# Eight padded projection tiles and 32-row scores in the first of two attention layers, pairs placed by the runs that close in the second

## The chip, the core and the metric

The program runs on one core of a Trainium2 chip. A core has engines that run side by side, each with its own queue of instructions in order: TensorE (PE) multiplies matrices from SBUF into PSUM banks; ScalarE (ACT) evaluates functions, here above all the exponential; VectorE (DVE) does elementwise work, reductions and copies out of PSUM; GpSimd (POOL) does elementwise work in SBUF; SyncE (SP) issues DMA transfers. The metric is the device time of one execution in microseconds. The kernel before took 1752.12 us, the median of three runs from 1749.59 to 1755.61.

## What is computed

Two layers, each an attention block and a token-mixing MLP, over one sequence of 2048 tokens of 640 features. Weights are shared by both layers.

```python
def _A_ref(x, wqkv, wo):                     # B, S, D, H = 1, 2048, 640, 32; Dh = 20
    qkv = (x @ wqkv).reshape(B, S, 3, H, Dh).transpose(2, 0, 3, 1, 4)
    q, k, v = qkv[0], qkv[1], qkv[2]
    scores = jnp.einsum("bhqd,bhkd->bhqk", q, k) * (Dh ** -0.5)
    p = _softmax(scores, axis=-1)
    o = jnp.einsum("bhqk,bhkd->bhqd", p, v)
    return o.transpose(0, 2, 1, 3).reshape(B, S, D) @ wo

def _B_ref(x, w1, b1, w2, b2):               # F = 1536
    h = _layernorm(x, axis=-1)
    u = _gelu(jnp.einsum("bsd,sf->bdf", h, w1) + b1)
    return (jnp.einsum("bdf,fs->bds", u, w2) + b2).transpose(0, 2, 1)

x = x + _A_ref(_layernorm(x), A_wqkv, A_wo)
x = x + _B_ref(_layernorm(x), B_w1, B_b1, B_w2, B_b2)
# and both once more
```

## The kernel before

**Scores and exponentials.** The 32 heads form 8 groups of four. The keys of a group are a tile of `KT` with 128 partitions: head `j` of the group has its 20 features in partitions 32j to 32j+19. Queries stand likewise in `QTq`, one block of 512 queries at a time, four blocks. A *unit* is one query block, one group and 128 keys: four *chunks* of 128 keys by 512 queries, one per head, each one matmul over 20 rows in its own strip of the array (`s_matmul`, lines 733 to 738). A chunk's exponential is done in one of two ways. ScalarE takes tiles of three and of two chunks in turn (`emit_exp`, line 806). VectorE takes chunks two at a time, a *pair*: one step from PSUM to integers (L576), then a polynomial and an addition of exponent bits (L617, L622, L641 or L643), with POOL doing two of the steps where it can (L694, L677). Each layer has 2048 chunks. `ve_admit` (from line 533) decides which chunks become pairs: it picks a unit `n` some way ahead of the cursor, by VectorE's planned backlog.

**Sums over keys.** `emit_PV` (L1466) multiplies the exponentials with the values into one bank `acc`. A *run* is a query block and a group, 16 units; when it closes, VectorE transposes the bank (L843), adds a partial sum where there is one, divides and transposes back (`finish_run`).

**The order is planned.** The Python code writes out every engine's order from modelled costs: `pem["t"]`, `dvm["t"]` and `acm["t"]` are the planned times of TensorE, VectorE and ScalarE. The order is then fixed; on the chip engines wait for one another by semaphores. Between score and value matmuls TensorE gets *fills* (projections, transposes, output and MLP matmuls; `add_fill`, `fill_step`), by priority and subject to gates, each evacuated by VectorE or ScalarE. Where the activity planned in a window of `SPAN_US` is under a floor (`wanting`, line 300), it gets *filler waves*, four matmuls of ones with zeros (L795). A fill matmul of 512 columns and a filler wave count 1 cell, a score chunk 0.25, whatever its rows.

**Hidden projections.** Each strip of 32 partitions has 12 unused ones. The kernel before projects five tiles (`NP`), not eight: the features of groups 5, 6 and 7 lie in the gaps of tiles 0 to 4, as `HIDDEN` says (tile, first gap row, rows, first feature). After the projection, DMAs on SyncE's queue carry them to their places (`carry`, L1215; `move_keys`, `move_queries`). The weights in the gaps are put there once, in the first layer, by 14 POOL copies (`gap_copies`, L1698), for groups 1 to 3 ahead of their first projection. Tile 0 is needed before that; its first projection runs with zeros in the gaps, and a second one of the same columns (`apart_fill`) goes to a separate tile, from where its pieces are moved.

**The opening of the first layer** (`TokenFeed.begin`). Input tiles of 128 tokens are loaded, normalised, transposed (L1357) and projected, four of them for each block of keys. Attention starts with *early runs*: groups 0 to 3 of query blocks 0 and 1, over the keys there are; their partial sums are kept in the key tiles 4 to 7 (`homes`), which can be filled only when the owner's early runs are done. SyncE issues in order: input tiles 0 to 3, the first halves of the key and query weights, half of the value weights, the second halves, input tiles 4 and 5, and the rest as buffers come free. Groups 0 to 3 of the weights are padded by ScalarE, group 4 by VectorE (L1735, L1737).

**The close of a layer** (`end_tiles`). The last two token tiles are finished apart; then the MLP's second product starts (`mixer_head`, L1942, L1955, L1964) with `w2s` blocks loaded ahead (L1977). The MLP's first product adds up in rows of `uacc`; `mid_rows` says for how many of its 12 rows four token tiles are added early.

**The second layer** (`MixFeed`) is fed by the MLP of the first. Until its feed has ended, pairs work in the upper half of `QTq` (`lent`, `new_w`), so fewer are in flight, and queries of groups 4 to 7 wait for it (`given_back`).

## Time and profile before

| quantity | us |
|---|---|
| median of three runs | 1752.12 |
| the profiled execution | 1746.78 |
| its span in the trace | 1745.0 |
| TensorE busy | 1672.1 |
| ScalarE busy | 1658.2 |
| VectorE busy | 1563.2 |
| POOL busy | 598.1 |

The profile is of one execution. A row of a group of instructions gives line, engine, operation, output and input tiles, shape and count, then busy time and the mean of one in ns, then the engine's idle time before them and what ended it. A row of a timeline gives start, duration, engine, line and count; in brackets stands the idle time before it and the work that ended it. A row of stretches gives the stretch, its length, each engine's busy time (PE, weight loads, VectorE, ScalarE, POOL; instructions in parentheses), the granted TensorE clock as a share of full speed, the DMA share and GB/s. Means of overlapping instructions on one engine can add up to more than its busy time.

### The profile page before, as it was taken

To read this page: it belongs to the slowest core of one execution; us is meant where nothing else is said; L and a number is where in the kernel's file an instruction comes from. 1 tells how busy PE (TensorE), PEld (TensorE's weight loads), DVE (VectorE), ACT (ScalarE), POOL (GpSimd) and SP (SyncE) were. 2 spreads that over 40 slices of the span, in tenths; PEclk is the share of its full clock that TensorE was granted. 3 is DMA by queue.
4 is the path that set the end of the run, shared out by engine and by line. 5 is a ranking of instruction groups with operands and counts; after the bars stand their busy time and mean duration, and the time that the engine had idled before them with its cause. 6 is when DMAs were issued, how large, how long until landed. Compare 5 with 4: busy or idle time off the path is not lost.

```text
span 1745.0 us, 44737 instructions
## 1 busy us (share of the span) xinstructions
PE 1672.1 (96%) x18414; PEld 659.0 (38%) x18414; DVE 1563.2 (90%) x2538; ACT 1658.2 (95%) x1488; POOL 598.1 (34%) x966
## 2 busy tenths in 40 slices
PE   8999999999999999999999999999999999999999
PEld 3333333333333344444534333333333333444445
DVE  7699999999999999998658669999999999999973
ACT  8999999999999999999789999999999999999970
POOL 4143333343544333342003113334335443434310
PEclk9999999999999999999999999999999999999999
DMA  5000000010122002023322011001002220211345
GB/s 130 24 13 1 16 14 2 15 39 3 51 60 81 20 28 68 6 76 110 113 81 75 25 57 21 11 2 51 18 15 81 70 62 2 69 53 30 79 121 178
DMA packets 107998, 85.91 MB, mean 49 GB/s; under 512 B 53504, under 2 KB 91952, under 8 KB 107792
## 3 DMA queue, kind: packets, MB, share of 16 engines
q1 hardware_dynamic: 102256, 75.16, 14.9%
q0 software_dynamic: 5536, 7.88, 1.5%
q8 instruction: 144, 2.36, 0.6%
q14 instruction: 62, 0.51, 0.1%
HBM read 55.48 MB, written 23.59 MB: 45 GB/s over the span
## 4 chain that ended last, share of the span: by engine, by line
ACT 48%; issue 22%; PE 21%; DVE 6%; DMA 1%; POOL 1%; SPq 0%; ACTq 0%; DVEq 0%; POOLq 0%
ACT P L806 48%; PE S L736 6%; PE acc L1466 3%; PE ya L1955 2%; PE acc L795 2%; PE misc L1304 1%; PE misc L1108 1%; DVE ey L622 1%; DVE ew L576 1%; PE um L1942 1%; DVE ey L617 1%; PE ya L1964 1%; PE misc L1333 1%; PE yb L1955 1%; PE Dt L1304 1%
## 5 line engine op out<-in xcount | busy, mean ns | idle before, releaser
L806 ACT ACTIVATE P<-S 128x1536 bf16<-128x1536 f32 (+1 forms) x1421 | 1609.2, 1355 | 17.3 <-PE S L736 16.1
L736 PE MATMUL S<-QTq,KT 20*128 20x512 bf16 (+1 forms) x4434 | 575.2, 338 | 55.9 <-ACT P L806 40.0
L694 POOL TENSOR_SCALAR ey<-ew 128x512 f16<-128x512 uint16 x508 | 313.9, 618 | 616.6 <-DVE ey L622 256.2
L736 PEld LDWEIGHTS <-KT 20*128 20x128 bf16 x5136 | 225.7, 91 | 519.7 <-issue 492.8
L795 PE MATMUL acc<-zr,zw 128*32 128x512 bf16 x4928 | 378.3, 382 | 1.2 <-POOL zr L160 1.2
L576 DVE TENSOR_SCALAR ew<-Dt 128x512 int32<-128x512 f32 x524 | 357.2, 682 | 23.3 <-PE Dt L736 14.1
L1466 PE MATMUL acc<-P,Vaug 128*32 128x512 bf16 (+1 forms) x4418 | 371.4, 344 | 0.1
L622 DVE SCALAR_TENSOR_TENSOR ey<-ey,ew 128x1024 int16<-128x1024 f16 x262 | 327.5, 1250 | 2.0
L677 POOL TENSOR_SCALAR Pd<-ew 128x512 int16<-128x512 int16 x304 | 187.2, 617 | 229.9 <-DVE ey L622 73.9
L736 PE MATMUL Dt<-QTq,KT 20*128 20x512 bf16 (+1 forms) x702 | 209.8, 334 | 0.0
L617 DVE TENSOR_TENSOR ey<-ey 128x1024 f16<-128x1024 f16 x273 | 195.2, 715 | 2.2 <-POOL ey L694 0.6
L795 PEld LDWEIGHTS <-zw 128*32 128x32 bf16 x5220 | 129.8, 96 | 116.0 <-issue 63.9
L1466 PEld LDWEIGHTS <-Vaug 128*32 128x32 bf16 x5120 | 104.1, 94 | 183.5 <-issue 169.8
L643 DVE SCALAR_TENSOR_TENSOR Pd<-ew,ey 128x512 int16<-128x512 int16 (+1 forms) x145 | 141.1, 973 | 0.0
L641 DVE TENSOR_TENSOR Pd<-Pd,ey 128x1024 int16<-128x1024 int16 (+1 forms) x197 | 124.0, 630 | 4.8 <-POOL Pd L677 2.8
L1466 PE MATMUL acc<-Pd,Vaug 128*32 128x512 bf16 (+1 forms) x702 | 107.5, 338 | 1.5 <-DVE Pd L641 1.1
L936 POOL TENSOR_TENSOR rstd<-veps,mhalf 128x1 f32<-128x1 f32 x60 | 47.8, 797 | 111.2 <-DVE veps L934 92.8
L1108 PEld LDWEIGHTS <-w1st 128*128 128x128 bf16 x672 | 53.0, 97 | 61.3 <-issue 49.1
L1108 PE MATMUL misc<-x1last,w1st 128*128 128x320 bf16 x384 | 73.0, 302 | 0.0
L1157 PE MATMUL misc<-wo_pad,attnT 128*128 128x320 bf16 x384 | 71.7, 302 | 0.8 <-DVE xin L1169 0.6
L843 DVE STREAM_TRANSPOSE T<-acc 128x512 f32<-128x512 f32 (+1 forms) x82 | 56.9, 694 | 11.9 <-PE acc L1466 11.7
L1108 PE MATMUL misc<-hh,w1st 128*128 128x320 bf16 x280 | 51.4, 301 | 1.4 <-DVE hh L1116 0.6
(157 smaller groups left out, 1200.4 us busy)
## 6 DMA issues: line engine op xcount, KB each, us to landing
w2s<-in_B_w_dram SPq DMA_DIRECT2D x16, 768.0 KB
uacc<-ustg POOLq DMA_DIRECT2D x24, 320.0 KB, 2.5
x1in<-xd SPq DMA_DIRECT2D x24, 320.0 KB
...
```

Of the source, the lines that this page charges most:

```text
L576: nc.vector.tensor_scalar(out=w[:, slot, :], in0=Dt[:, :], scalar1=127.0 * FIX, scalar2=0.0, op0=ALU.add, op1=ALU.max)
L617: nc.vector.tensor_tensor(out=y, in0=y, in1=y, op=ALU.mult)
L622: nc.vector.scalar_tensor_tensor(out=box["t"][:, 0:512 * k], in0=y[:, 0:512 * k], scalar=MANT_C * MANT_K ** 2, in1=frac, op0=ALU.add, op1= ...
L641: nc.vector.tensor_tensor(out=bits, in0=bits, in1=t, op=ALU.add)
L643: nc.vector.scalar_tensor_tensor(out=bits, in0=whole[:, lo:hi], scalar=128.0, in1=t, op0=ALU.mult, op1=ALU.add)
L677: after_vector(nc.gpsimd.tensor_scalar(out=bits, in0=whole, scalar1=128.0, scalar2=0.0, op0=ALU.mult, op1=ALU.add))
L694: return engine.tensor_scalar(out=out_ap, in0=in_ap, scalar1=MANT_K / FIX, scalar2=-MANT_K * MANT_S, op0=ALU.mult, op1=ALU.add)
L736: pe(nc.tensor.matmul(out_ap[:, c0:c0 + w], lhsT=KT[32 * j:32 * j + DH, g, kt * 128:(kt + 1) * 128], rhs=get_QT(st, qb)[32 * j:32 * j + DH ...
L795: pe(nc.tensor.matmul(bank[32 * j:32 * j + 32, 0:w], lhsT=zw[:], rhs=zr[:, :, 0:64].to_broadcast([128, w // 64, 64]), start=start, stop=st ...
L806: nc.scalar.activation(out=P[:, 0:ncs, :].rearrange("p a b -> p (a b)"), in_=St[:, 0:ncs, :].rearrange("p a b -> p (a b)"), func=ACT.Exp, ...
L1108: pe(nc.tensor.matmul(t[:, 0:w], lhsT=w1_of[(p, ft)][:, sti, :], rhs=rows_in[sti][:, c0:c1], start=(sti == 0), stop=(sti == n_in - 1)))
L1466: pe(nc.tensor.matmul(acc[32 * j:32 * j + 32, a0:a0 + w], lhsT=Vaug[:, (kt * H + hh_) * VW:(kt * H + hh_) * VW + 32], rhs=P[:, slot, c0:c0 ...
```

## The change

In the first layer all eight groups are projected as tiles of their own with zeros in the gaps. Tiles 5 to 7 of the weights are in a new pool (`w_over`) that lives as long as the layer. Its scores are matmuls over 32 rows, the 12 rows of zeros included. There are no moves and no separate copy of tile 0 in this layer. At its close `fold` copies the weights of groups 5 to 7 into the gaps of tiles 0 to 4 (14 POOL copies), for the second layer, which keeps five tiles, moves and 20 rows. The second halves of the key and query weights are loaded after input tile 5's normalisation. Groups 4 to 7 are padded by VectorE. ScalarE and VectorE zero the gaps. The order of late groups and the homes of partial sums in the first layer are now 6, 7, 4, 5. `mid_rows` of the first layer is 0.

A score chunk now counts its rows over 128 in the planned activity (0.25 in the first layer, 20/128 in the second), and the floors are per layer, 0.04 lower in the second. In the second layer the unit for a new pair is moved on by the number of closed runs that still have units pending before it, over 1.8.

```diff
-    FLOOR=0.52,
-    FLOOR_RUN=0.68,
+    FLOOR=(0.52, 0.48),
+    FLOOR_RUN=(0.68, 0.64),
...
-    apart = []
+    w_over = []
+
+    def w_of(i, g):
+        return (wk_pad, wq_pad)[i][:, :, g, :] if g < NP else w_over[i][:, :, g - NP, :]
+
+    def quads(ap):
+        return ap.rearrange("p a (j i) -> p a j i", i=32)
+
+    def fold(i, L, tile_, first, n, dim):
+        nc.gpsimd.tensor_copy(out=quads(w_of(i, tile_))[:, :, :, DH + first:DH + first + n],
+                              in_=quads(w_of(i, L))[:, :, :, dim:dim + n])
...
-        homes = {EQ[0]: (4, 6), EQ[1]: (5, 7)}
-        rest = [6, 4, 5, 7]
+        homes, rest = feed.homes, feed.rest
...
-                if len(ve_procs) > 2 or feed.lent and not late and any(q.pair < p - 1 for q in ve_procs):
+                if len(ve_procs) > 2 or feed.nested and not late and any(q.pair < p - 1 for q in ve_procs):
                     return
                 done = backlog(now) + 2 * 1.2 + 4.0 + CFG["VE_MARGIN"]
                 n = max(cursor[0] // NH + max(CFG["VE_LEAST"], math.ceil(done / 1.8)), ve_state["unit"] + 1)
+                if feed.nested:
+                    n += math.ceil(sum(r["closed"] and bool(r["pending"]) and r["pending"][-1] < n
+                                       for r in runs[pv_run[0]:]) / 1.8)
...
-            at = pe_wave("S", cells=0.25) if clash else now
+            at = pe_wave("S", cells=cells_s) if clash else now
...
             for kt, q0, w, c0 in parts:
-                pe(nc.tensor.matmul(out_ap[:, c0:c0 + w], lhsT=KT[32 * j:32 * j + DH, g, kt * 128:(kt + 1) * 128],
-                                    rhs=get_QT(st, qb)[32 * j:32 * j + DH, g, q0:q0 + w], start=True, stop=True,
+                pe(nc.tensor.matmul(out_ap[:, c0:c0 + w], lhsT=KT[32 * j:32 * j + feed.rows, g, kt * 128:(kt + 1) * 128],
+                                    rhs=get_QT(st, qb)[32 * j:32 * j + feed.rows, g, q0:q0 + w], start=True, stop=True,
                                     tile_position=(32 * j, 0)))
...
-
-        def apart_of(i, tile_, tb):
-            return apart[i] if feed.regap and tile_ == 0 and tb == 0 else None
...
-            if feed.regap and L == 5:
-                need.append(("G", 0))
...
             def issue():
                 for tile_, first, n, dim in HIDDEN[L]:
-                    cut = 512 if apart_of(0, tile_, 0) is not None else 0
-                    if cut:
-                        carry(KT[:, L, :], apart[0], 0, cut, first, n, dim)
-                    carry(KT[:, L, :], KT[:, tile_, :], cut, S, first, n, dim)
-                at = moved_at(L, need, 8 if feed.regap and L == 5 else 0)
+                    carry(KT[:, L, :], KT[:, tile_, :], first, n, dim)
...
-        def apart_fill(i, prio):
-            wpad = (wk_pad, wq_pad)[i]
...
-            def evac(t, end, eng):
-                copy_on(eng, apart[i][:], t[:, :], q_scale if i else None)
-
...
         def proj_fill(kind, g, tb, prio, ready, gate=None, fed=False):
-            if g >= NP:
+            if feed.nested and g >= NP:
                 return
-            if kind == "Q" and g >= EG:
+            if feed.nested and kind == "Q" and g >= EG:
                 gate1 = gate
                 gate = lambda: given_back(tb) and (gate1 is None or gate1())
-            wpad, key = (wk_pad, ("K", g, tb)) if kind == "K" else (wq_pad, ("Q", tb, g))
-            if feed.regap:
-                wi = int(kind == "Q")
-                mark = (wi, "gap0") if g == 0 and tb > 0 else (wi, g)
-                gate0 = gate
-                gate = lambda: mark in cx.w_at and (gate0 is None or gate0())
+            wpad, key = (w_of(0, g), ("K", g, tb)) if kind == "K" else (w_of(1, g), ("Q", tb, g))
...
-                    if tb == 0:
+                    if feed.nested and tb == 0:
                         for L in HIDDEN:
                             move_keys(L)
                             move_queries(L, 0)
-                        if feed.regap:
-                            for i in range(2):
-                                apart_fill(i, when(4, 0) - 4)
-                    for g in range(NP):
+                    for g in (*range(EG), *rest):
...
+        if not feed.nested:
+            for i in range(2):
+                for L, parts in HIDDEN.items():
+                    for p in parts:
+                        fold(i, L, *p)
...
-        regap = True
-        lent = False
+        nested = False
+        rows = 32
+        homes = {0: (6, 7), 1: (4, 5)}
+        rest = (6, 7, 4, 5)
...
-        mid_rows = 2
+        mid_rows = 0
...
             load_w(self.wv[:, 0], 2 * D)
-            load_raw(0, 1)
-            load_raw(1, 1)
             for tt in range(4, 6):
                 load_x(tt)
 
             def load_rest():
+                load_raw(0, 1)
+                load_raw(1, 1)
                 load_w(self.wv[:, 1], 2 * D + D // 2)
             landing = {tt: 3.2 + 0.5 * tt for tt in range(4)}
-            landing.update({4: 12.0, 5: 12.5})
+            landing.update({4: 9.5, 5: 10.0})
 
-            def gap_of(i, tile_, first, n):
-                return wpads[i][:, :, tile_, :].rearrange("p a (j i) -> p a j i", i=32)[:, :, :, DH + first:DH + first + n]
-            cx.submit(cx.Proc(0, [(0.2, lambda e, i=i: nc.vector.memset(gap_of(i, 0, 0, GAP), 0.0), 0.0) for i in range(2)], 0.9))
...
-            gaps_at(10.8, [(0, 1)])
-            gaps_at(12.0, [(1, 1), (0, 2), (1, 2), (0, 3), (1, 3)])
-            gaps_at(19.0, [(0, 4), (1, 4)])
-            gaps_at(19.0, [(0, 0), (1, 0)], lambda: ("K", 0, 0) in cx.kready and ("Q", 0, 0) in cx.kready)
+            def pads(i, part):
+                w = (wpads[i][:, :, 0:4, :], wpads[i][:, :, 4:NP, :], w_over[i][:])[part]
+                return w.rearrange("p a g (j i) -> p a (g j) i", i=32)[:, :, :, DH:32]
+            cx.submit(cx.Proc(0, [(0.46, lambda e, i=i: nc.vector.memset(pads(i, 0), 0.0), 0.0) for i in range(2)], 0.9))
 
...
-                              [], 2.1, eng=cx.acm))
+                              [((0.2, 0.42)[part - 1], lambda e, i=i, part=part: nc.scalar.memzero(pads(i, part)), -0.06)
+                               for i in range(2) for part in (1, 2)],
+                              2.1, eng=cx.acm))
...
-            for g in range(NP):
+            for g in range(NG):
...
     class MixFeed:
         groups = 4
-        regap = False
-        lent = True
+        nested = True
+        rows = DH
+        homes = {0: (4, 6), 1: (5, 7)}
+        rest = (6, 4, 5, 7)
...
     with ExitStack() as a_stack:
+        over = a_stack.enter_context(tc.tile_pool(name="w_over", bufs=1))
+        w_over.extend(over.tile([128, NDT, NG - NP, 128], BF16, name=f"w_over{i}") for i in range(2))
```

105 lines of the change are left out of this document (33 added, 72 removed).

## Prediction

> **What bounds the kernel now.** I read the page first, then busy time by stretches, then ScalarE's timeline alone, because its exponentials run nearly without a break.
>
> ```profile
> span 1745.0 us, 44737 instructions
> ...
> L806 ACT ACTIVATE P<-S 128x1536 bf16<-128x1536 f32 (+1 forms) x1421 | 1609.2, 1355 | 17.3 <-PE S L736 16.1
> ```
> ```profile
> 40.00:60.00 20.00, 19.96 (x127) 6.08 (x119) 9.03 (x21) 17.18 (x15) 1.11 (x2) 0.80 0.16 37
> 60.00:80.00 20.00, 18.84 (x158) 6.42 (x156) 15.93 (x28) 20.00 (x19) 4.57 (x8) 0.97 0.04 11
> ...
> 200.00:300.00 100.00, 97.08 (x1188) 31.63 (x1180) 97.95 (x146) 100.00 (x90) 33.55 (x55) 1.00 0.05 8
> ...
> 1000.00:1100.00 100.00, 94.35 (x828) 35.60 (x827) 81.42 (x147) 98.72 (x88) 26.32 (x43) 0.98 0.14 35
> ```
>
> The columns of the second view are PE, PEld, DVE, ACT, POOL, granted clock, DMA share, GB/s. In steady state (200 to 300 us) ScalarE works 100.00 of 100 us and VectorE 97.95: both are full, so the time is the number of score chunks (one head, 128 keys, 512 queries) divided by what the two do together. TensorE's 97.08 is no bound there, since it holds filler matmuls (below). The exception is the first layer's opening (40 to 60): ScalarE 17.18 of 20, VectorE 9.03, clock 0.80. A small copy of it is at 1000 to 1100 (98.72, clock 0.98). ScalarE's timeline gives each break, in brackets:
>
> ```profile
> 16.23 22.83 ACT L806 ACTIVATE P<-S 128x1536 bf16<-128x1536 f32 x20 [3.10 <-PE S L736]
> 39.60 2.53 ACT L806 ACTIVATE P<-S 128x1536 bf16<-128x1536 f32 x2 [0.54 <-PE S L736]
> 43.26 2.52 ACT L806 ACTIVATE P<-S 128x1536 bf16<-128x1536 f32 x2 [1.13 <-PE S L736]
> 47.37 34.17 ACT L806 ACTIVATE P<-S 128x1536 bf16<-128x1536 f32 x30 [1.58 <-PE S L736]
> 82.61 255.57 ACT L806 ACTIVATE P<-S 128x1536 bf16<-128x1536 f32 x226 [1.08 <-PE S L736]
> ...
> 1071.63 3.28 ACT L806 ACTIVATE P<-S 128x1024 bf16<-128x1024 f32 x3 [0.42 <-PE S L736]
> 1075.77 269.31 ACT L806 ACTIVATE P<-S 128x1536 bf16<-128x1536 f32 x238 [0.86 <-PE S L736]
> ```
>
> So: 3.10 us before the first exponential, 0.54 + 1.13 + 1.58 = 3.25 at 39 to 47, 1.08 at 82, 0.42 + 0.86 = 1.28 at 1071 to 1076. These are what the change can win; work added to a full engine is what it can lose.
>
> **Part by part: the start.** The second halves of the key and query weights are now loaded after the input tiles that the start needs, not before them, and the six small gap copies ahead of groups 1 to 3 go.
>
> ```profile
> 11.43 0.52 POOL L1698 COPY wq_pad<-w_raw 128x160 bf16<-128x160 bf16 x2 [0.61 <-DMA w_raw<-in_A_wqkv_dram]
> ...
> 11.70 1.24 PE L1304 MATMUL misc<-hh,wq_pad 128*128 128x512 bf16 x5
> ...
> 11.88 0.49 DVE L919 BATCH_NORM_STATS2 bnst<-x0in 128x6 f32<-128x320 bf16 x1 [0.75 <-DMA x0in<-in_A_x_dram]
> ...
> 13.60 0.49 DVE L919 BATCH_NORM_STATS2 bnst<-x0in 128x6 f32<-128x320 bf16 x1 [0.83 <-DMA x0in<-in_A_x_dram]
> 14.01 0.67 DVE L385 CAST KT<-Dt 128x512 bf16<-128x512 f32 x1
> ...
> 15.07 0.67 DVE L387 TENSOR_SCALAR QTq<-misc 128x512 bf16<-128x512 f32 x1
> ```
>
> VectorE's queue holds the statistics of input tiles 4 and 5 ahead of the key evacuation; they wait for their loads (0.75 and 0.83 us), the second ending at 13.60. Thus the keys, whose matmuls stand ahead of the queries' on TensorE, are drained only at 14.01, and the queries, done at 11.70 + 1.24 = 12.94, at 15.07. The last of the two weight halves landed by 11.43, 0.45 before tile 4 did; with them gone, tiles 4 and 5 land ahead of that. Then the keys drain at about 12 and the queries at about 13.1, bound now by their own matmuls. From that cast to the first exponential took 16.23 − 15.07 = 1.16 us, so the first exponential comes near 14.2. **−2.0 us**; ends 0 (something else in that queue is late instead) and −3.1 (the whole break). The new zeroing on ScalarE is two weights of 120 and 360 words each, 960 in all:
>
> ```profile
> 2.12 1.11 ACT L1720 ACTIVATE Vaug<-Vaug 128x1024 uint32<-128x1024 uint32 x1
> ```
>
> At 1024 words in 1.11 us that is about 1.2 us with four instructions; part falls in idle time before the input arrives, part delays a transpose's evacuation: **+0.3** (0 to +1.2). VectorE's larger zeroing stands first in its queue, ahead of the first input's arrival: nothing.
>
> **The moves.** The first layer's moves of hidden projections go: seven pieces of four DMAs each for the keys (four more for the separate copy of tile 0) and for each of four query blocks, 144 DMAs. They share SyncE's queue with the input tiles, and stand ahead of two of them here:
>
> ```profile
> 34.86 2.70 SPq L1215 DMA_DIRECT2D QTq<-QTq  x4
> ...
> 37.66 0.86 SPq L1672 DMA_DIRECT2D x0in<-in_A_x_dram  x2
> ...
> 39.96 0.49 DVE L919 BATCH_NORM_STATS2 bnst<-x0in 128x6 f32<-128x320 bf16 x1 [2.26 <-DMA x0in<-in_A_x_dram]
> ```
> ```profile
> 36.00:38.00 2.00, 1.33 (x17) 0.47 (x16) 1.70 (x4) 2.00 (x3) 0.41 (x1) 0.98 1.23 17
> 38.00:40.00 2.00, 2.00 (x21) 0.38 (x13) 0.04 (x1) 1.46 (x3) 0.00 (x0) 0.50 1.20 173
> ...
> 1072.00:1075.00 3.00, 3.00 (x23) 0.80 (x14) 2.20 (x3) 2.91 (x3) 0.62 (x1) 0.53 0.15 25
> ```
>
> Four moves hold the queue from 34.86; tiles 14 and 15 are issued at 37.66, and VectorE stands still 2.26 us for them until 39.96. Behind it waits an evacuation, behind that the bank, and TensorE's order behind the bank. TensorE was busy 1.33 of 2 us just before, and the clock went to 0.50; the 0.80 over 40 to 60 is 0.50 for 8 us of it. The three breaks of 3.25 us lie in that stretch. Without moves the tiles can go out some 2.8 us sooner, and VectorE's wait of 2.26 is covered; next in line to be late are the output weights' loads in the same queue. **−3.0** (0 to −3.25). The break at 82 us has no load ahead of it, only a clock at half; scores with 32 rows instead of 20 might hold the clock. I take **−0.5** (0 to −1.08).
>
> [...]
>
> **The added projections.** Eight tiles for keys and queries over four blocks are 64 evacuations; now there are 40 and 2 for the separate copy, so 22 more, each with five matmuls. VectorE also copies eight weight groups, not two.
>
> ```profile
> L795 PE MATMUL acc<-zr,zw 128*32 128x512 bf16 x2608 | 200.0, 384 | 1.2 <-POOL zr L160 1.2
> L576 DVE TENSOR_SCALAR ew<-Dt 128x512 int32<-128x512 f32 x284 | 193.7, 682 | 14.6 <-PE Dt L736 9.7 <-PE S L736 0.7
> L622 DVE SCALAR_TENSOR_TENSOR ey<-ey,ew 128x1024 int16<-128x1024 f16 x142 | 176.6, 1243 | 1.3
> ...
> L617 DVE TENSOR_TENSOR ey<-ey 128x1024 f16<-128x1024 f16 x142 | 100.6, 708 | 1.2
> ...
> L641 DVE TENSOR_TENSOR Pd<-Pd,ey 128x1024 int16<-128x1024 int16 x59 | 44.6, 755 | 1.4 <-POOL Pd L677 1.0
> ...
> L387 DVE TENSOR_SCALAR QTq<-misc 128x512 bf16<-128x512 f32 x18 | 12.2, 680 | 1.1 <-PE misc L1304 1.1
> ```
> ```profile
> L1737 DVE COPY wk_pad<-w_raw 128x400 bf16<-128x400 bf16 x1 | 0.2, 231 | 0.0
> ```
>
> Evacuations: 22 × 0.680 = 15.0 us. Copies: 6 × 0.23 = 1.4. The change of `mid_rows` from 2 to 0 takes away four evacuations of 320 columns, by width 320/512 × 0.68 = 0.43 each, −1.7. Sum 14.7 us on VectorE. One pair of chunks there costs 2 × 0.682 + 1.243 + 0.708 + 0.755 = 4.07, a chunk 2.04 us; ScalarE takes 1609.2 / (1421 × 2.5) = 0.453. Together they do 0.49 + 2.21 = 2.70 chunks a microsecond, so 14.7 us of VectorE cost 14.7 × 0.49 / 2.70 = **+2.7 us**. Ends: 0, if all fits VectorE's idle time before 100 us (10.97 of 20 and 4.07 of 20 above), unlikely, since key tiles 4 to 7 hold the early runs' partial sums until those end; +3.3, if every chunk displaced (14.7/2.04) falls to ScalarE alone. On TensorE 110 matmuls at 1.24 / 5 are 27 us; they count in the planner as one cell each, as a filler wave does, and replace fillers, of which this layer has 200 us. Without that cover they would cost up to 27 us, but then ScalarE could not be at 100.
>
> **The fold and the layout.** Fourteen POOL copies at the close; the same shapes ran early in the layer, and the close looks like this:
>
> ```profile
> L1698 POOL COPY wk_pad<-w_raw x7: 243/321/387, 10.3 to 22.1; 128x240 bf16<-128x240 bf16 x3, 128x160 bf16<-128x160 bf16 x2, 128x80 bf16<-128x80 bf16 x2
> ```
> ```profile
> 841.67 0.55 POOL L936 TENSOR_TENSOR rstd<-veps,mhalf 128x1 f32<-128x1 f32 x1 [15.75 <-DVE veps L934]
> ```
> ```profile
> 817.26 3.24 SPq L1977 DMA_DIRECT2D w2s<-in_B_w_dram  x2
> ```
> ```profile
> 829.42 0.38 PE L1964 MATMUL ya<-uT,w2s 128*128 128x512 bf16 x1
> ```
>
> 14 × 0.32 = 4.5 us inside 15.75 us in which POOL has nothing: **0**; without that cover 4.5. Behind it on POOL stand the second layer's zeroing of `T2` and that row's `rstd`, for which a normalisation waits; only the second layer's projections read the result itself. The 7.7 KB per partition of extra weights push the pools up, so the first `w2s` block now lies over exponential tiles read until the end and goes out near 820.5, not 817.26. Its first reader is at 829.42; the second block's issue already ended at 817.26 + 3.24 = 820.50. **0**. `mid_rows` 0 leaves 16 more matmuls near the end, in place of fillers: 0.
>
> **The second layer.** Pairs are chosen later by one unit or two where closed runs are pending. The row for that is a late pair:
>
> ```profile
> 1070.81 0.39 PE L1466 MATMUL acc<-Pd,Vaug 128*32 128x512 bf16 x2 [1.10 <-DVE Pd L641]
> ```
> ```profile
> L576 DVE TENSOR_SCALAR QTq<-Dt 128x512 int32<-128x512 f32 x22 | 15.0, 682 | 6.0 <-PE Dt L736 5.6
> ...
> L576 DVE TENSOR_SCALAR ew<-Dt 128x512 int32<-128x512 f32 x10 | 6.7, 674 | 0.1
> ```
>
> TensorE waited 1.10 us for a pair's result while VectorE finished a closing run; the clock fell to 0.53 and ScalarE lost the 1.28 us. **−0.9** (0 to −1.28). The floors fall by 0.04 while scores count 20/128, not 0.25, per chunk: per 3.413 us window at 2.70 chunks/us, 9.2 chunks count 0.86 cells less and the floor asks 0.64 cells less (16 cells × 0.04), so 0.2 more filler waves, nothing on ScalarE. The same rule can also refuse pairs; that is the rival below.
>
> **Sum.** −2.0 + 0.3 − 3.0 − 0.5 + 2.7 − 0.9 = −3.4 us, against the profiled execution's 1746.78 (span 1745.0, so 1.8 around it): 1743.4. That execution is 5.3 below the median of the three timed, 1752.12, so I carry the difference, not the value: 1748.7.
>
> **Rivals.** *Pairs are lost in the second layer* (slower). Between 893 and 1075 us 22 + 10 chunks went to VectorE, which is not full there (81.42 of 100). A chunk refused costs ScalarE 0.453 us and nothing comes back. The later unit must already be within reach of the projections, which are still being made in that stretch. It decides from 8 chunks on (3.6 us, the whole gain); 24 lost give 10.9, net +7.5: 1759.6. Against it: the shift is one or two units. Chance 0.22.
>
> *The opening fills up* (faster). With the tiles earlier, VectorE's idle 10.97 + 4.07 us between 40 and 80 takes pairs: 15.0 / 2.04 = 7 chunks, 3.3 us off ScalarE, sum −6.7: 1745.4. For it: a VectorE idle for half of 40 to 60. Against: the planner admits pairs by its own clock, which never saw the loads' lateness. Chance 0.25.
>
> [...] Chance 0.18. [...]
>
> **How the numbers follow.** The forecast has 0.35, its own range 1745 to 1752 by the ends of its terms. About 0.3%, 5.3 us, is what a measurement tells from no change: faster is below 1746.8. The faster rival gives 0.22 to faster, the forecast 0.14: 0.36. Slower takes 0.19 from the first rival and 0.02 from the third: 0.21. The rest, 0.43, is the same. The range runs from 1741 (the faster rival with the full ends of the start, of 82 us and of the second layer's break, 1.1 + 0.6 + 0.4, and 2 us of scatter, a third of the 6.0 between the three timed runs) to 1760 (24 chunks lost).
>
> **What would show it.** First exponential near 14.2 us; no granted clock of 0.50 between 36 and 50; ScalarE above 19.5 of 20 in 40 to 60; first-layer chunks on VectorE down from 284 by about 7; no wait for a pair's result at a close in the second layer; the pairs' count between the second layer's start and 1075 still 32 chunks. Wrong would be: breaks of ScalarE over 1 us at new places in 100 to 250, where the added evacuations fall, or fewer than 24 of those 32 chunks.

## The result, and the profile after

| | before | after |
|---|---|---|
| median of 8 executions each, side by side | 1748.52 (1742.3 to 1755.6) | 1738.84 (1737.7 to 1741.2) |
| the profiled execution | 1746.78 | 1737.74 |
| its span | 1745.0 | 1736.0 |
| first layer's exponentials, first start to last end | 16.23 to 820.10: 803.87 | 15.14 to 814.72: 799.58 |
| second layer's exponentials | 856.53 to 1675.58: 819.05 | 851.26 to 1666.48: 815.22 |

The ratio is 0.9945 with a 95% interval of 0.9926 to 0.9964: faster by half a per cent, and by more than the forecast, whose 1748.7 stood for 3.4 us less and whose range ended at 1741. The profiled executions differ by 9.0 us, in three pieces: the first exponential starts 1.1 us earlier, the first layer's exponentials take 4.3 us less, the second layer's 3.8. The close between the layers (36.4 and 36.5 us from the last exponential to the next layer's first) and the tail (69.4 and 69.5) are as they were. The last column of the first row says something else too: before scatters over 13 us, after over 3.5.

ScalarE's timeline after (start, duration, line, count, in brackets the break before). All breaks over 0.2 us of the first layer behind its first exponential are gone, and so is the pair at 1071 to 1076; the largest that is left, 3.92 us, stood in the kernel before with the same length:

```profile
15.14 606.43 ACT L818 ACTIVATE P<-S 128x1536 bf16<-128x1536 f32 x536 [1.94 <-PE S L748]
621.76 192.96 ACT L818 ACTIVATE P<-S 128x1536 bf16<-128x1536 f32 x171 [0.19 <-ACT P L818]
...
880.23 7.38 ACT L818 ACTIVATE P<-S 128x1024 bf16<-128x1024 f32 x7 [3.92 <-PE S L748]
888.02 296.65 ACT L818 ACTIVATE P<-S 128x1536 bf16<-128x1536 f32 x262 [0.42 <-PE S L748]
1184.83 481.65 ACT L818 ACTIVATE P<-S 128x1536 bf16<-128x1536 f32 x426 [0.16 <-PE acc L1440]
```

The stretches after (PE, PEld, VectorE, ScalarE, POOL, clock, DMA share, GB/s). The clock is 1.00 where it was 0.80, ScalarE works 19.99 of 20 us, and VectorE is busier in 60 to 80 (18.23, before 15.93) and in 1000 to 1100 (84.78, before 81.42):

```profile
40.00:60.00 20.00, 19.25 (x142) 6.85 (x144) 9.81 (x19) 19.99 (x19) 1.39 (x3) 1.00 0.10 23
60.00:80.00 20.00, 18.68 (x166) 6.72 (x165) 18.23 (x32) 20.00 (x19) 6.21 (x10) 1.00 0.06 18
...
1000.00:1100.00 100.00, 94.47 (x824) 35.24 (x826) 84.78 (x151) 100.00 (x90) 26.50 (x42) 1.00 0.15 36
```

Now the term that was forecast as a loss, the added projections. The first layer's groups on VectorE and POOL, 15 us to the layer's end, before and after (output and input tiles, shape, count, busy time, mean ns):

```profile
L643 DVE SCALAR_TENSOR_TENSOR Pd<-ew,ey 128x512 int16<-128x512 int16 (+1 forms) x83 | 78.7, 949 | 0.0
...
L385 DVE CAST KT<-misc 128x512 bf16<-128x512 f32 x15 | 10.2, 681 | 5.5 <-PE misc L1304 5.4
```
```profile
L677 POOL TENSOR_SCALAR Pd<-ew 128x512 int16<-128x512 int16 x162 | 99.9, 617 | 130.5 <-DVE ey L622 36.1 <-DVE ey L617 22.5 <-DVE Pd L643 17.6
```
```profile
L588 DVE TENSOR_SCALAR ew<-Dt 128x512 int32<-128x512 f32 x282 | 191.9, 680 | 13.3 <-PE Dt L748 10.0
...
L655 DVE SCALAR_TENSOR_TENSOR Pd<-ew,ey 128x512 int16<-128x512 int16 (+1 forms) x66 | 66.0, 999 | 0.0
L395 DVE CAST KT<-misc 128x512 bf16<-128x512 f32 x27 | 18.4, 680 | 3.2 <-PE misc L1279 3.2
L397 DVE TENSOR_SCALAR QTq<-misc 128x512 bf16<-128x512 f32 x27 | 18.4, 680 | 1.1 <-PE misc L1279 0.9
```
```profile
L689 POOL TENSOR_SCALAR Pd<-ew 128x512 int16<-128x512 int16 x179 | 110.5, 620 | 132.4 <-DVE ey L634 40.4 <-DVE ey L629 19.9 <-PE S L748 14.4
```

The evacuations came as forecast (key casts from that bank 15 to 27, queries 18 to 27). But VectorE still does 282 chunks (284 before): POOL took 17 more of the pairs' additions (179, before 162), and VectorE's own additions in the first row fell by 12.7 us. Without the four breaks of 4.33 us the first layer's exponentials took 799.54 us before, and 799.58 after, so in these two profiles the added work cost nothing. The plan lets POOL start such a piece beside a VectorE instruction of 0.45 us or more, unless it marks that instruction as one that keeps POOL out, as it does a pair's own steps behind the first; each added evacuation is such a host.

### The profile page after: what moved, and what is told of

Read it like the earlier page. It is cut to its first block, busy times and chain, and to the rows that moved or that the text cites. A ratio compares the mean times of both kernels' runs of the same rounds, so it can differ in the third digit from the quotient of the medians.

```text
span 1736.0 us, 43779 instructions
## 1 busy us (share of the span) xinstructions
PE 1653.5 (95%) x17971; PEld 662.4 (38%) x18043; DVE 1570.4 (90%) x2547; ACT 1657.4 (95%) x1492; POOL 608.7 (35%) x979
## 4 chain that ended last, share of the span: by engine, by line
ACT 52%; issue 23%; PE 23%; DVE 1%; DMA 0%; SPq 0%; POOL 0%; another core or an unknown queue 0%; ACTq 0%; DVEq 0%; POOLq 0%
ACT P L818 52%; PE S L748 6%; PE acc L1440 3%; PE ya L1908 2%; PE acc L807 2%; PE misc L1279 2%; PE misc L1120 1%; PE um L1895 1%; PE Dt L1279 1%; PE ya L1917 1%; PE misc L1169 1%; PE yb L1908 1%; PE misc L1827 1%; PE Dt L1827 0%; PE misc L1310 0%
## 5 line engine op out<-in xcount | busy, mean ns | idle before, releaser
L748 PE MATMUL S<-QTq,KT 32*128 32x512 bf16 (+3 forms) x4429 | 575.1, 336 | 65.6 <-ACT P L818 49.4
L748 PEld LDWEIGHTS <-KT 32*128 32x128 bf16 (+1 forms) x5131 | 231.0, 91 | 521.4 <-issue 492.2
L588 DVE TENSOR_SCALAR ew<-Dt 128x512 int32<-128x512 f32 x522 | 355.3, 681 | 23.1 <-PE Dt L748 16.3
L1440 PE MATMUL acc<-P,Vaug 128*32 128x512 bf16 (+1 forms) x4418 | 365.0, 343 | 0.5 <-issue 0.3
L807 PE MATMUL acc<-zr,zw 128*32 128x512 bf16 x4516 | 346.1, 383 | 1.4 <-POOL zr L159 1.2
L689 POOL TENSOR_SCALAR Pd<-ew 128x512 int16<-128x512 int16 x317 | 195.7, 620 | 232.4 <-DVE ey L634 60.7
L748 PE MATMUL Dt<-QTq,KT 32*128 32x512 bf16 (+3 forms) x702 | 209.8, 334 | 0.0
L807 PEld LDWEIGHTS <-zw 128*32 128x32 bf16 x4744 | 118.6, 96 | 102.1 <-issue 53.8
L655 DVE SCALAR_TENSOR_TENSOR Pd<-ew,ey 128x1024 int16<-128x1024 int16 (+1 forms) x129 | 130.8, 1014 | 0.0
```

Of the source, the lines that this page charges most:

```text
L588: nc.vector.tensor_scalar(out=w[:, slot, :], in0=Dt[:, :], scalar1=127.0 * FIX, scalar2=0.0, op0=ALU.add, op1=ALU.max)
L655: nc.vector.scalar_tensor_tensor(out=bits, in0=whole[:, lo:hi], scalar=128.0, in1=t, op0=ALU.mult, op1=ALU.add)
L689: after_vector(nc.gpsimd.tensor_scalar(out=bits, in0=whole, scalar1=128.0, scalar2=0.0, op0=ALU.mult, op1=ALU.add))
L748: pe(nc.tensor.matmul(out_ap[:, c0:c0 + w], lhsT=KT[32 * j:32 * j + feed.rows, g, kt * 128:(kt + 1) * 128], rhs=get_QT(st, qb)[32 * j:32 * ...
L807: pe(nc.tensor.matmul(bank[32 * j:32 * j + 32, 0:w], lhsT=zw[:], rhs=zr[:, :, 0:64].to_broadcast([128, w // 64, 64]), start=start, stop=st ...
L1440: pe(nc.tensor.matmul(acc[32 * j:32 * j + 32, a0:a0 + w], lhsT=Vaug[:, (kt * H + hh_) * VW:(kt * H + hh_) * VW + 32], rhs=P[:, slot, c0:c0 ...
```

## The experiments

Changes are to the kernel after unless it says "before". All ratios are to the kernel before, run beside them. The changed kernel itself stood beside the others in the series of `after_again` and `after_b` only.

**The mark.** Twice the changed kernel itself, in two series.

> The changed kernel itself, unchanged, as the mark for the others beside it. First profile: span 1736.0, first exponential 15.14, last exponential of the first layer ends at 814.72, second layer 851.26 to 1666.48. Expected again within 1.5 us, the start of the first exponential within 1 us (the three runs with its start otherwise unchanged had 15.6 to 16.2), and no clock under 0.99 between 40 and 150 us.

> The changed kernel a third time, as the mark beside the other three on this chip. Expected: 1737.7 to 1740 in nearly all executions (its 12 timed before lay in 1737.7 to 1739.8), first exponential between 15.1 and 16.2, no clock under 0.96 from 40 to 150 us.

1738.09 us (0.9957, 0.9944 to 0.997) and 1738.8 us (0.9967, 0.9955 to 0.998). The first exponential came at 15.59 and 15.58, the first layer's exponentials took 799.6 both times, the second's 815.2. So 15.14 in the first profile was early by about half a microsecond.

**Rows.** Only the width of the first layer's scores, the order unchanged:

```diff
-    lhsT=KT[32 * j:32 * j + feed.rows, g, kt * 128:(kt + 1) * 128],
-    rhs=get_QT(st, qb)[32 * j:32 * j + feed.rows, g, q0:q0 + w]
+    lhsT=KT[32 * j:32 * j + DH, g, kt * 128:(kt + 1) * 128],
+    rhs=get_QT(st, qb)[32 * j:32 * j + DH, g, q0:q0 + w]
```

> The changed kernel with the same order of every engine, but the first layer's score matmuls read 20 rows of keys and queries, not 32 (the 12 rows left out are zeros, so the scores are the same). Theory 'rows': the clock of the matmul engine follows the rows that work, and 32 rows hold it; then stretches at about 0.5 come back in the first layer's opening (36 to 100 us), with breaks of ScalarE there of 1 to 4 us in all (before: 4.33), span 1737 to 1740. Rival 'loads': the clock dropped because input tiles 14 and 15 came late behind the moves; then the clock stays 1.00 throughout and the span is within 0.5 us of 1736.0.

> Again the changed kernel with first-layer scores over 20 rows, now beside the changed kernel on one chip. Theory 'rows': its executions scatter upwards (1738.9 to 1747.7 in the first series), median 2 to 3 us over the changed kernel's, and the profile shows breaks of about 1 us with a clock under 1.00 in 60 to 110 us. Rival 'chance': median within 0.7 us and the same scatter as the changed kernel beside it.

1740.77 us (1738.89 to 1747.67; 0.9973, 0.9956 to 0.999), and in the second series 1745.37 (1737.8 to 1751.22; 0.9988, 0.9969 to 1.0008), where the changed kernel beside it took 1738.8 (1738.2 to 1740.1). Four of its twelve executions there are as short as the changed kernel's, eight are 6 to 12 us longer. The profile of the first series has a clock of 0.96 over 60 to 100 us and of 0.97 over 100 to 150, with breaks of 1.00 and 1.04 us. That of the second series shows more. ScalarE's timeline, then the stretches of this run and those of the changed kernel beside it:

```profile
15.84 22.70 ACT L818 ACTIVATE P<-S 128x1536 bf16<-128x1536 f32 x20 [2.02 <-PE S L748]
38.77 2.47 ACT L818 ACTIVATE P<-S 128x1536 bf16<-128x1536 f32 x2 [0.23 <-PE S L748]
42.90 2.36 ACT L818 ACTIVATE P<-S 128x1536 bf16<-128x1536 f32 x2 [1.66 <-PE S L748]
46.30 2.53 ACT L818 ACTIVATE P<-S 128x1536 bf16<-128x1536 f32 x2 [1.03 <-PE S L748]
50.06 2.37 ACT L818 ACTIVATE P<-S 128x1536 bf16<-128x1536 f32 x2 [1.24 <-PE S L748]
52.72 25.33 ACT L818 ACTIVATE P<-S 128x1536 bf16<-128x1536 f32 x22 [0.28 <-PE S L748]
79.06 29.48 ACT L818 ACTIVATE P<-S 128x1536 bf16<-128x1536 f32 x26 [1.02 <-PE S L748]
109.59 520.30 ACT L818 ACTIVATE P<-S 128x1536 bf16<-128x1536 f32 x460 [1.04 <-PE Dt L748]
```
```profile
36.00:38.00 2.00, 1.67 (x13) 0.60 (x10) 2.00 (x6) 2.00 (x3) 0.00 (x0) 0.86 1.59 161
38.00:40.00 2.00, 2.00 (x9) 0.49 (x8) 1.28 (x4) 1.77 (x2) 0.00 (x0) 0.50 1.06 103
40.00:60.00 20.00, 19.97 (x127) 5.79 (x125) 6.28 (x16) 15.58 (x15) 1.11 (x2) 0.72 0.11 25
```
```profile
36.00:38.00 2.00, 1.67 (x18) 0.76 (x15) 2.00 (x6) 2.00 (x3) 0.00 (x0) 1.00 1.71 136
38.00:40.00 2.00, 2.00 (x24) 0.64 (x23) 2.00 (x8) 2.00 (x3) 0.30 (x1) 1.00 0.83 105
40.00:60.00 20.00, 19.63 (x146) 6.84 (x143) 9.43 (x18) 19.99 (x18) 1.43 (x3) 1.00 0.10 24
```

The matmuls and their order are the same, VectorE is full (2.00 of 2) and waits for no load. With 20 rows the clock is 0.86 over 36 to 38 us and 0.50 over 38 to 40, with 32 it is 1.00 in both. (That TensorE is busy 1.67 of 2 us in both is an accident: a clock of 0.86 over these 2 us is 0.56 us at 0.50, so with 20 rows part of them already ran at half clock.) The breaks from 38 to 110 us add up to 6.5 us; they are like those of the kernel before, at nearly the same places.

This pair of profiles alone does not settle that rows are the cause, because profiles differ in where the clock falls. In the profile before it was at 0.50 for 10.24 us from 37.93, for 3.41 us from 78.89 and for 3.41 us from 1072.17; in that of the second series it was under 1.00 in 36 to 60, 60 to 80 and 100 to 150 us and 1.00 over 1000 to 1100. Nor does the busy share alone decide: at 36 to 38 us TensorE was busy 1.33 of 2 us in the kernel before, whose clock fell, and 1.35 of 2 in the kernel before with eight buffers (below), whose clock stayed at 1.00. What settles it is the number of executions. The mean clock of a whole execution was 0.997 or less in 12 of 24 with 20 rows (the two series here), and 0.998 or more in all 27 of the changed kernel and in all 24 of the two runs on VectorE work below, which stood beside the first series. The profiles point the same way: between 36 and 150 us the clock fell in 4 of the 8 with 20-row scores there and in 1 of the 10 with 32 rows (the run without the second layer's rule, below: 0.97 over 100 to 150). Two other kernels with 32 rows had a mean clock of 0.997 or less too, in 5 of 12 executions (halves first, below; in its profile 0.75 over 16 to 18 us, 0.50 over 18 to 20 and 0.99 over 850 to 1000) and in 4 of 12 (without the rule; 0.97 over 100 to 150 and 0.98 over 1000 to 1100).

Thus 32 rows held the clock in the executions of the changed kernel, and 20 rows lost it in half of them. The kernel before scatters by that, and by falls at about 1070 us in the second layer, whose scores keep 20 rows (below).

**Late input tiles, in the kernel before.** The forecast put the breaks at 39 to 47 us down to tiles 14 and 15 standing behind moves. Four runs. First these tiles from POOL's queue:

```diff
-                nc.sync.dma_start(out=xin[tt][:], ...)
+                (nc.gpsimd if tt >= 14 else nc.sync).dma_start(out=xin[tt][:], ...)
```

> The kernel before, but its input tiles 14 and 15 are loaded from POOL's queue, not from SyncE's behind the moves; the rest is as before. Theory 'loads behind the moves' (the step of the prediction): VectorE's wait of 2.26 us until 39.96 goes, the breaks at 39 to 47 us (3.25 us) go with it and the clock of 0.50 there; span 1745.0 less 2.5 to 3.3. Rival 'rows' (20-row scores cannot hold the clock in the opening, whenever the tiles come): the wait goes, but a stretch of clock 0.50 and breaks of 1 us or more stay between 36 and 110 us, and the gain is under 2 us.

1747.33 us, 1.0012 (0.9991 to 1.0033). VectorE's wait was gone, but breaks of 1.08 and 1.53 us stayed with the clock at 0.83 in 40 to 60. It tells little: the first exponential came late, at 17.23, and POOL's loads and memsets got in VectorE's way themselves (one normalisation took 1.79 us). That second effect was in the kernel before too. VectorE's normalisations there, POOL beside them, and the same normalisations in the next run, where POOL's memsets end at 33.43 and its loads come later:

```profile
34.17 2.38 DVE L940 TENSOR_SCALAR h_bf<-x0in,mv,rstd 128x640 bf16<-128x640 bf16 x2
...
36.87 0.43 DVE L940 TENSOR_SCALAR h_bf<-x0in,mv,rstd 128x640 bf16<-128x640 bf16 x1
```
```profile
34.12 1.18 POOL L196 MEMSET wo_pad<- 128x1280 f32 x1
35.23 1.18 POOL L191 DMA_DIRECT2D b_t<-in_B_b_dram  x1
```
```profile
34.66 0.45 DVE L940 TENSOR_SCALAR h_bf<-x0in,mv,rstd 128x640 bf16<-128x640 bf16 x1 [0.65 <-PE misc L1357]
...
35.42 0.44 DVE L940 TENSOR_SCALAR h_bf<-x0in,mv,rstd 128x640 bf16<-128x640 bf16 x1
...
39.33 0.49 DVE L919 BATCH_NORM_STATS2 bnst<-x0in 128x6 f32<-128x320 bf16 x1 [3.07 <-DMA x0in<-in_A_x_dram]
```

Two instructions of 0.43 us took 2.38 while POOL cleared a buffer and issued a load. (The memset started 0.05 us ahead of them. Which part the memset has in it and which the load, no run separates.) So the bias loads were moved behind those normalisations (`bias`), six input buffers made eight so that the tiles go out ahead of the moves (`x8`), and both:

```diff
-                nc.gpsimd.dma_start(out=b1_t[:], ...)
+                after_vector(nc.gpsimd.dma_start(out=b1_t[:], ...))
...
-                    if tt in (9, 11):
-                        setup_bias(tt // 2 - 4)
+                    if tt == 11:
+                        setup_bias(0), setup_bias(1)
...
-            self.xp = stack.enter_context(tc.tile_pool(name="x0p", bufs=6))
+            self.xp = stack.enter_context(tc.tile_pool(name="x0p", bufs=8))
...
-            for tt in range(4, 6):
+            for tt in range(4, 8):
                 load_x(tt)
...
-                        load_x(tt + 6)
+                        tt + 8 < NT and load_x(tt + 8)
```

> The kernel before, with POOL's two loads of the MLP's biases issued after the normalisation of input tile 11, not between its memsets at 32.9 to 36.4 us; every compute engine's order is the same. In the trace before, VectorE's normalisations took 2.38 us for two (0.43 each elsewhere) while POOL worked. Theory 'POOL blocks': they take 0.9 us, TensorE is busy 1.67 of 2 us or more at 36 to 38, the clock of 0.50 and the breaks at 39 to 47 us (3.25) are gone or under 1 us. Rival 'loads': VectorE waits longer for tiles 14 and 15 (3 to 4 us, not 2.26) and the breaks stay.

> The kernel before with eight buffers for input tiles, not six, so that tiles 14 and 15 are issued ahead of the moves on SyncE's queue; the order of the compute engines is the same. Theory 'loads' (the step of the prediction): VectorE's wait of 2.26 us goes, with it the clock of 0.50 at 38 to 46 and the 3.25 us of breaks. Rival 'POOL blocks': the wait goes, but the clock still falls and 2 us or more of breaks stay, as in the run with these tiles on POOL's queue (1.08 and 1.53 us).

> Both changes of the two runs beside it. 'Loads' and 'POOL blocks' alike: no clock under 0.9 between 36 and 60, breaks at 39 to 47 under 0.6 us, span about 3 us shorter than before. Rival 'rows': with both waits gone the 20-row scores and the same matmuls still let the clock fall there, 2 us or more of breaks stay.

With the bias moved, the wait for the tiles grew to 3.07 us as its rival said (above), two breaks of 0.74 and 0.41 us stayed, and the clock did not fall (1.00 from 34 to 150 us). With eight buffers the first layer had no break over 0.2 us and a clock of 1.00 from 34 to 150 us, though TensorE was busy only 1.35 of 2 us at 36 to 38 and POOL still held VectorE for 2.38:

```profile
15.88 316.82 ACT L806 ACTIVATE P<-S 128x1536 bf16<-128x1536 f32 x280 [1.86 <-PE S L736]
332.87 481.75 ACT L806 ACTIVATE P<-S 128x1536 bf16<-128x1536 f32 x426 [0.17 <-ACT P L806]
```

With both, the clock held from 36 to 60 us (1.00) and there was no break there; one of 1.15 us stood ahead of 19.66.

The medians are 1745.5 (0.9989, 0.9973 to 1.0005), 1745.22 (0.998, 0.9964 to 0.9995) and 1741.95 (0.9975, 0.996 to 0.9991), each scattering over 8 to 12 us as 20 rows do. By these profiles I put the late tiles at 1.2 us (0.74 + 0.41) in an execution whose clock holds, and the remaining 2.1 of the 3.25 us down to the clock. POOL's blocking alone cannot be told from nothing here. These are single profiles of kernels whose clock falls by chance, so that split is an estimate.

**What VectorE work costs.** One run takes away POOL's piece under the 24 evacuations of groups 5 to 7, one does each of them twice (the second copy writes the same values). In the diff `bare` marks a step that hosts no POOL piece; the last two lines are the other run's:

```diff
+                key = grp["key"]
+                extra = layer == 0 and (key[0] == "K" and key[1] >= NP or key[0] == "Q" and key[2] >= NP)
...
+                proc.bare = (1,) if extra else ()
...
+                if extra:
+                    steps.insert(0, (grp["cost"], lambda end: grp["evac"](t, end, eng), 0.0))
```

> The changed kernel, but in the first layer POOL is given no piece of a pair's work while VectorE evacuates a key or query projection of groups 5 to 7 (24 evacuations). Theory 'POOL pays': the added evacuations cost little because POOL takes an addition of exponent bits under each (179 such pieces in the first layer, 162 before; VectorE's own additions 66.0 us against 78.7). Then about 17 pieces go back to VectorE (12.7 us), which at 0.49 of 2.70 chunks per us is +2.3 us; chunks on VectorE in the first layer fall from 282 by about 6. Rival 'idle time pays' (VectorE's idle time before 100 us took pairs, 13 chunks there and 11 before): POOL finds its pieces under other instructions, 174 to 184 of them, and the span is within 0.5 us of 1736.0.

> The changed kernel, with each of the 24 evacuations of key and query projections of groups 5 to 7 in the first layer done twice by VectorE (16.3 us more work there, same result). The forecast's price (0.49 of 2.70 chunks per us): +3.0 us, 8 chunks fewer on VectorE. Theory 'POOL pays': about 18 more additions go to POOL (0.75 us of VectorE each), 2.8 us are left, +0.5 us, and 1 to 2 chunks fewer.

Without the cover: 1742.09 us (0.9977, 0.9964 to 0.999), first-layer exponentials 15.61 to 817.41, 801.8 us, 2.2 more than the 799.6 of the changed kernel's profiles. POOL's groups of pair work in that run (the changed kernel had 273 and 179):

```profile
L708 POOL TENSOR_SCALAR ey<-ew 128x512 f16<-128x512 uint16 x263 | 162.6, 618 | 329.2 <-DVE ey L636 113.5 <-DVE Pd L657 71.9 <-DVE ey L631 60.1
L691 POOL TENSOR_SCALAR Pd<-ew 128x512 int16<-128x512 int16 x165 | 101.7, 619 | 150.0 <-DVE ey L636 40.2 <-DVE Pd L657 23.7 <-DVE ey L631 20.4
```

24 pieces fewer, one for each of the 24 evacuations, VectorE 280 chunks instead of 282, and breaks of 0.40 and 0.17 us at about 224 us. Idle time did not pay instead: from 16 to 815 us VectorE was busy 758.3 us in the run with eight buffers and 758.5 in `after_b`, two profiles without breaks. The forecast of this run (2.3 us) held in time and in additions lost (14 of 17), not in chunks (2, not 6). Twice: 1743.92 us (0.9988, 0.9974 to 1.0003), 15.61 to 817.68, 802.1 us, 2.5 more, and 278 chunks. (Its median is higher by more than that: in its profile the close between the layers took 38.7 us, not 36.5, and the second layer's exponentials took 816.9, 1.7 more, with a clock of 0.99 over 850 to 1000 us.) The run was expected at +0.5 us if POOL paid for these too; its additions rose only from 179 to 181, so a second copy right behind the first hosts nothing, and the price is that of bare work. 16.3 us of bare VectorE work thus cost 2.5 us, 0.15 us for each, where the forecast's price was 0.49 / 2.70 = 0.18.

**The start.** The halves of the weights put back ahead of input tiles 4 and 5, and a later planned landing of these tiles:

```diff
-            for tt in range(4, 6):
-                load_x(tt)
-
-            def load_rest():
-                load_raw(0, 1)
-                load_raw(1, 1)
+            load_raw(0, 1)
+            load_raw(1, 1)
+            for tt in range(4, 6):
+                load_x(tt)
+
+            def load_rest():
```
```diff
-            landing.update({4: 9.5, 5: 10.0})
+            landing.update({4: 11.0, 5: 11.5})
```

> The changed kernel with one thing put back: the second halves of the key and query weights are loaded before input tiles 4 and 5, as in the kernel before; the order of all compute engines is the same. Theory 'loads of the start': tiles 4 and 5 come 1.5 to 2.1 us later (first statistics at 11.9 and 13.6, as before, not 9.75 and 11), the first exponential at 16.2 to 16.7 (15.14 in the changed kernel), span +1.1 to +1.6. Rival 'the start has another bound' (the query projection, which waited for a bank): first exponential within 0.2 us of 15.14.

> The changed kernel with the planned landing of input tiles 4 and 5 at 11.0 and 11.5, not 9.5 and 10.0, so that their statistics stand behind the first value evacuation in VectorE's queue (it ran at 11.66, 1.1 us after its matmuls, and held a bank that the query projection needs), and with the bias loads later as in the runs beside it. Theory 'start held by the bank': first exponential 0.5 to 1 us sooner than the 15.1 to 16.2 of the changed kernel's runs, time 1737.0 to 1737.6. Rival: the start scatters with the arrival of the first input, nothing changes, 1738.1 as beside the same chip's runs before.

> The changed kernel with the planned landing of input tiles 4 and 5 at 11.0 and 11.5 alone. With the bias loads moved too it began its exponentials at 14.61 and took 1737.9. Theory 'start held by the bank': first exponential 14.5 to 15.0, 0.5 to 1 us under the changed kernel's median beside it. Rival: no difference beyond 0.3 us, since the later order gives it back.

With the halves first: 1743.36 us (0.9986, 0.997 to 1.0002). The loads of the start bound it, and by more than expected (19.05 against 15.6; the rest of the median is partly the second layer, with a clock of 0.99 over 850 to 1000 us and a break of 1.09 us ahead of 891.17): tile 4's statistics began at 12.80 after a wait of 3.15 us, the value evacuation behind them at 14.71, TensorE starved (0.58 of 2 us at 12 to 14), the clock was 0.75 over 16 to 18 and 0.50 over 18 to 20, and the first exponential came at 19.05. Its statistics, then the changed kernel's VectorE in that stretch, then the value evacuation with the later landing (`a_land`):

```profile
12.80 0.49 DVE L931 BATCH_NORM_STATS2 bnst<-x0in 128x6 f32<-128x320 bf16 x1 [3.15 <-DMA x0in<-in_A_x_dram]
```
```profile
9.75 0.49 DVE L931 BATCH_NORM_STATS2 bnst<-x0in 128x6 f32<-128x320 bf16 x1 [0.39 <-DMA x0in<-in_A_x_dram]
...
10.56 0.48 DVE L931 BATCH_NORM_STATS2 bnst<-x0in 128x6 f32<-128x320 bf16 x1
...
11.66 0.45 DVE L395 CAST Vaug<-misc 128x320 bf16<-128x320 f32 x1
...
13.19 0.69 DVE L395 CAST KT<-Dt 128x512 bf16<-128x512 f32 x1
13.79 0.68 DVE L397 TENSOR_SCALAR QTq<-misc 128x512 bf16<-128x512 f32 x1
```
```profile
11.27 0.49 DVE L395 CAST Vaug<-misc 128x320 bf16<-128x320 f32 x1 [0.54 <-ACT hh L391]
```

In the changed kernel both tiles' statistics stand ahead of the value evacuation, which empties the bank that the query projection needs. With the later landing that evacuation ran at 11.27 between the two, and the first exponential came at 14.84 alone and 14.61 with the bias loads moved. `a_land` took 1737.42 us (1736.8 to 1739.0; 0.9959, 0.9946 to 0.9973), its span 1735.6 against 1736.4 of the changed kernel beside it. It is the shortest median of all, 1.4 us under the changed kernel's, though the intervals of the two ratios overlap. With the bias loads too 1737.9 (0.9938, 0.9922 to 0.9954); it gave back 1.02 us in a break at 1180 that the run without them does not have.

**The second layer.** The rule taken out, the floors and counts put back, and the rule alone put into the kernel before (with eight buffers):

```diff
-                if feed.nested:
-                    n += math.ceil(sum(r["closed"] and bool(r["pending"]) and r["pending"][-1] < n
-                                       for r in runs[pv_run[0]:]) / 1.8)
```
```diff
-    FLOOR=(0.52, 0.48),
-    FLOOR_RUN=(0.68, 0.64),
+    FLOOR=(0.52, 0.52),
+    FLOOR_RUN=(0.68, 0.68),
...
-        cells_s = feed.rows / 128
+        cells_s = 0.25
```

> The changed kernel without the new rule by which a pair of the second layer is placed later where runs close. Second layer's exponentials took 819.05 us before and 815.22 after (-3.83; its breaks of 1.28 us at 1071 to 1076 are gone). Theory 'rule': all of that is the rule: the breaks by a late pair come back (1 to 1.5 us), VectorE has 2 chunks fewer (262), 818 to 819 us. Rival 'floors': the rule gives only the break of 1.28 us or less, 815.5 to 816.5, and the rest comes from the lower floors and the smaller count of a score.

> The changed kernel with the second layer's floors (0.52, 0.68) and its count of a score (0.25) as before. Theory 'rule': nothing on ScalarE's path changes, second layer within 0.4 us of 815.22. Rival 'floors': 816.5 to 818 us, VectorE 262 chunks.

> The kernel before with input tiles 14 and 15 issued ahead of the moves (eight buffers), and with the second layer's new rule for pairs. If these two are what the change won beside the rows: first layer as in the run with eight buffers (its exponentials 15.88 to 814.62, no break), second layer 815.2 to 815.8 instead of 818.2, span 1736 to 1737 in an execution without a fall of the clock; the median stays above the changed kernel's by the scatter that 20 rows leave (1 to 3 us). Rival: the second layer's gain hangs on the lower floors or on the other weights, 817 us or more.

| run | second layer's exponentials | us |
|---|---|---|
| kernel before | 856.53 to 1675.58 | 819.05 |
| before with eight buffers | 851.03 to 1669.25 | 818.22 |
| before with eight buffers and the rule | 854.74 to 1670.53 | 815.79 |
| after without the rule | 853.46 to 1671.14 | 817.68 |
| after with the old floors | 852.11 to 1667.53 | 815.42 |
| after | 851.26 to 1666.48 | 815.22 |

The rule is worth 2.4 us in the kernel before with eight buffers (818.22 − 815.79), with the clock at 1.00 over the layer on both sides. In the changed kernel it is 2.5 (817.68 − 815.22), but there the run without the rule had a clock of 0.98 over 1000 to 1100 us, and 0.88 of this is the break ahead of 1072.72. Without the rule that clock was 0.98 in three profiles (the kernel before, with tiles 14 and 15 on POOL's queue, and this run), each with such a break of 0.86 to 0.88 us; the other three have no such break, and with the rule none of 12 has. Over the same stretch the clock was 1.00 in 11 of these 12 (the twelfth, with the later landing and the bias loads moved, has 0.999 over the whole execution). The floors are worth 0.2. Of the kernel before's 819.05, 0.8 is its own fall at 1072.17 (0.50 for 3.41 us) with the break of 0.86 behind it, which the run with eight buffers did not have. The rest of the 3.83, about 0.4, has no run. Without the rule ScalarE breaks as before, and VectorE takes fewer chunks before 1075 (without the rule, then with it):

```profile
1068.55 3.28 ACT L815 ACTIVATE P<-S 128x1024 bf16<-128x1024 f32 x3 [0.42 <-PE S L745]
1072.72 210.39 ACT L815 ACTIVATE P<-S 128x1536 bf16<-128x1536 f32 x186 [0.88 <-PE S L745]
```
```profile
850.00:1075.00 225.00, 21.76 (x32) 0.99 0.17 53
```
```profile
850.00:1075.00 225.00, 25.13 (x37) 1.00 0.18 52
```

32 chunks against 37 up to there, and 262 against 264 in the whole layer. Two chunks at 0.453 us and the breaks of 1.30 us make 2.2 of the 2.46 us. The times: without the rule 1742.1 (0.9984, 0.9967 to 1.0), 1739.2 to 1752.9; this is also the one profile with 32 rows whose clock fell between 36 and 150 us, with a break of 1.08 us at 103. The row of 100 to 150 us:

```profile
100.00:150.00 50.00, 46.88 (x383) 16.72 (x378) 42.90 (x71) 48.92 (x45) 15.37 (x25) 0.97 0.05 11
```

With the old floors 1738.82 (0.9965, 0.9952 to 0.9978). The kernel before with eight buffers and the rule took 1740.46 (0.9975, 0.9963 to 0.9987), 1738.3 to 1747.1, beside the changed kernel's 1738.8: its shortest executions are as short, and the 20-row scatter is left. Its profile missed the expected span of 1736 to 1737 (1739.9), since tile 4 came late (statistics at 14.98) and the first exponential at 18.40.

## Why the prediction was wrong, step by step

Three steps carry the miss of 9.9 us: the price of the added projections (+2.7 forecast, 0 to 0.9 measured), the size of the second layer's gain (−0.9, measured −3.8), and the step from the profile to the median (5.3 carried, 1.1 measured). The terms for the start and for the breaks are off by less than 1 us each, in opposite directions.

- **Start**, −1.7 with the zeroing, in the range 0 to −3.1: −1.1 in the profile, about −0.6 by the two other runs (15.6). The loads did come earlier: tile 4's statistics began at 9.75 to 10.78 in nine profiles of the changed order, at 11.88 to 14.98 in six of the kernel before and its variants. But the first exponential came at 15.14 to 16.17 in the nine and at 15.63 to 18.40 in the six, by the medians 0.6 apart. "Then the keys drain at about 12 and the queries at about 13.1" is what failed: they drained at 13.19 and 13.79, because the statistics of tiles 4 and 5, now early, stand ahead of the value evacuation, and the query projection waits for its bank. Moving them behind it won 0.7 us more.
- **The moves**, −3.0: the breaks went (3.25), but by the estimate above only 1.2 us of them for the late tiles. With the tiles early and no moves, a profile with 20-row scores still had 6.5 us of breaks.
- **The break at 82 us**, −0.5 "scores with 32 rows instead of 20 might hold the clock": right as a guess (nothing in the forecast worked it out), and too small and too narrow. The rows help hold the clock from 36 to 110 us (over 40 to 60 it was 0.72 in the second series and 1.00 in the changed kernel beside it), and in the median they were worth 6.6 us beside the changed kernel (1745.37 against 1738.8), 2.7 in the other series (1740.77 against 1738.09, on another chip).
- **The added projections**, +2.7: the first step that failed. By chunks the loss was 2 (284 to 282), 0.9 us. Against the run of the kernel before that had no break (798.7 us of exponentials) the changed kernel's 799.6 are 0.9 longer; against the profile before without its breaks, nothing. "14.7 us of VectorE cost 14.7 × 0.49 / 2.70" prices bare VectorE work about right (0.18 us for each, measured 0.15), but an evacuation is not bare: POOL takes a piece of a pair beside each, which is worth 2.2 us over 24. The faster rival came near the size (+2.7 − 3.3 = −0.6 for this term and its own) but had the wrong place: VectorE's chunks before 100 us rose only from 11 to 13, and most of the added evacuations fell at 150 to 500 us, where VectorE is full.
- **The second layer**, −0.9 (0 to −1.28): the second step that failed. It counted the one break and took fewer pairs as the risk of the rule. The layer took 3.8 us less, 2.4 to 2.5 of them by the rule, with five chunks more, not fewer, before 1075. That pairs placed later finish in time for the next to be let in is my reading; no run separates it from the order that came with it.
- **Fold and layout**, 0: held. POOL copied at 820.61 to 824.75 and, behind one memset, was idle for 11.07 us. The `w2s` loads went out at 815.31, 0.6 us after the layer's last exponential and ahead of their first reader at 824.16, as argued (820.5 was 0.4 after the last exponential of the kernel before, 820.10).

```profile
820.61 2.23 POOL L209 COPY wk_pad<-w_over 128x240 bf16<-128x240 bf16 x7
822.77 1.98 POOL L209 COPY wq_pad<-w_over 128x240 bf16<-128x240 bf16 x7
...
836.41 0.55 POOL L948 TENSOR_TENSOR rstd<-veps,mhalf 128x1 f32<-128x1 f32 x1 [11.07 <-DVE veps L946]
```

- **From the profile to the median**: the third step that failed, and the largest. 5.3 us were carried over. The changed kernel's median lies 1.1 above its profile, because most of the scatter went with the clock's falls (its mean clock was 0.998 or more in all of these 8 executions); and eight executions of the kernel before had a median of 1748.5, not 1752.1. Of the 9.9 us between 1748.7 and 1738.84, 5.7 are the sum's (1743.4 against 1737.74) and 4.2 this step's.
